# Attention over memory slots, then a three-way maxout layer: both softmaxes subtract their maximum

## The chip, the cores and the metric

The kernel runs on one core of a Trainium2 chip. The metric is the device time of one execution in microseconds (us); the time before is the median of three runs. One further execution was profiled, and all durations below come from that one. Engines have short names: PE is TensorE (matmuls), PEld its weight loads, DVE is VectorE, ACT is ScalarE, POOL is GpSimd, SP is SyncE, which here only issues DMAs. L499 is line 499 of the kernel's source.

## The reference, cut to what matters

```python
# q, k, v: (8, 8, 576, 64)   phi: (8, 8, 576, 32)   all float32
a = np.exp(phi - np.max(phi, axis=2, keepdims=True))   # axis 2: the tokens
a = a / (np.sum(a, axis=2, keepdims=True) + 1e-09)
k_m = np.einsum('bhsm,bhsd->bhmd', a, k)
v_m = np.einsum('bhsm,bhsd->bhmd', a, v)
scores = 1.0 / np.sqrt(64) * np.matmul(q, k_m.transpose(0, 1, 3, 2))
scores = scores - np.max(scores, axis=-1, keepdims=True)   # over the 32 slots
attn = np.exp(scores)
attn = attn / (np.sum(attn, axis=-1, keepdims=True) + 1e-09)
y = np.matmul(attn, v_m)                     # (8, 8, 576, 64)
x = y.transpose(0, 2, 1, 3).reshape(4608, 512)
h = np.maximum(np.maximum(x @ w1, x @ w2), x @ w3)     # w1, w2, w3: (512, 768)
out = h @ w_out                                        # w_out: (768, 512)
```

The first softmax runs over the 576 tokens of a head, the second over its 32 memory slots. Neither maximum changes the value of its softmax in exact arithmetic.

## The kernel before, in words

A batch (one of 8) holds 8 heads as 4 pairs and 576 tokens. The instructions of all engines are issued in an order written out by hand: a list of short words such as `F4@1!`, a letter for a step, a number for its part, the batch behind the `@`, and `!` or `*` to move an evacuation of PSUM to the other engine or to both. Each engine takes its share of the list strictly in that order. PSUM is eight banks of 512 fp32 columns; which banks a step takes is written out too, as a string of digits.

The steps of a batch:

- `L0`, `L1`, `L2`, `L3` (in halves `H`, `J`) load phi, k, v and q (L108, L111, L125). They are issued from POOL and cast to bf16 on the way, except phi, which stays fp32; the first phi comes from SP (L106). Each of k, v and q of a batch is 1.18 MB in HBM, phi is 0.59 MB.
- `E` (L262) is exp of phi on ACT, `B` (L282) sums phi's exponentials with k, v and a column of ones on PE, `N` (L300 to L314) normalizes on DVE, `K` (L329) transposes the result on PE. `r` (L117) repacks k and v on POOL for batches 2 to 7.
- `Q` (L344) transposes q in 32 x 32 blocks on DVE. `S` (L364) makes the scores of the batch on PE, two groups of 128 rows (slots of four heads) by 576 tokens, and exponentiates them on ACT (L373) straight from PSUM into a bf16 tile e2.
- For each group: `a` (L418) transposes e2 in 32 x 32 blocks, pairs of bf16 moved as one 4-byte element (288 columns); `s` (L426) sums over slots; `c` (L435) takes the reciprocal; `m` (L440) multiplies on POOL; `X` (L448) transposes back into attn. Batch 0 does it otherwise: `M` (L385) multiplies e2 with a block matrix of ones on PE, `R` takes exp(-ln) of the sums on ACT (L397, L403), and `X` multiplies on DVE (L408).
- The values are folded into the weights. `W` and `O` (with `o` for a half) form w3 times w_out, `V` (L246) turns w1 and w2 into w1 - w3 and w2 - w3, and `D0` to `D4` (L471) multiply the batch's values v_m with columns of these, to wp, and with w3 w_out, to wp3 (`D3`). So x @ w1 - x @ w3 is attn @ wp. For batch 0 `D1` to `D4` take other column ranges and subtract w3 within the product.
- `F0` to `F11` (L499) are the first layer, 6 tiles of 128 columns for w1 (even) and w2 (odd); `f` issues the first half ahead. The w1 half is evacuated with a ReLU on ACT or DVE (L195, L199), the w2 half with a maximum on DVE (L523) into hT. Each takes two banks.
- `T0` to `T4` (L542 to L571) are the output tiles of 128 tokens: six products of hT with w_out and two of attn with wp3; `p` issues two of the six ahead. The tile is copied from PSUM by ACT or DVE and written by one DMA from SP of 128 rows (L583). T4 belongs to two batches. The very last tile (L594 to L615) is in two column parts, 384 by SP and 128 by ACT.

The weights come once: w3 (`Y2`, 1.57 MB), w_out (`y4`, `y5`, 0.79 MB each), w1 in two parts (`y0` with 512 columns, 1.05 MB, and `y1`, 0.52) and w2 (`y2` with 256 columns, 0.52, and `y3`, 1.05). `Z` issues warm-up products on PE.

Of the kernel before, what the change touches and what calls it, by code (L numbers as in the profile page):

```python
# [8 lines left out]
FP32 = mybir.dt.float32  # L9
BF16 = mybir.dt.bfloat16  # L10
AF = mybir.ActivationFunctionType
ALU = mybir.AluOpType
# [3 lines left out]
def kernel(  # L16
# [139 lines left out]
    blkones = const.tile([P, P], BF16, name="blkones")  # L156
    nc.vector.memset(blkones, 0.0)
    for i in range(P // M):
        nc.vector.memset(blkones[M * i : M * (i + 1), M * i : M * (i + 1)], 1.0)
# [6 lines left out]
            02010240624567675420624062402640240264526720426206260402602460264301466410462046  # L166
            20462402472640320642026502642064026401460246046024604264026401462040640264026402
            64206420560272046042704624602642604264024062602032323232
# [85 lines left out]
    ln = const.tile([P, S], FP32, name="ln")  # L254
    ONES = {(0, 0), (0, 1)}
    st = {}

# [93 lines left out]
    def att_score(b):  # L351
# [3 lines left out]
        e2 = s["e2"] = work.tile([P, NG, S], BF16, name="e2")  # L355
# [16 lines left out]
        for a in range(NG):  # L372
            nc.scalar.activation(  # L373
                out=e2[:, a].rearrange("p (t r c) -> p t r c", t=2, c=NC),
                in_=sc[a][:, :, 0:SH].rearrange("p t (c r) -> p t r c", c=NC),
                func=AF.Exp,
                scale=0.125,
            )

    def ones_sum(b, g):  # L380
        s = st[b]
        e2 = s["e2"]
        sm = two_banks()
        for h in range(2):
            nc.tensor.matmul(  # L385
                sm[:, h, 0:SH],
                lhsT=blkones,
                rhs=e2[:, g, h * SH : (h + 1) * SH],
                start=True,
                stop=True,  # L390
            )
        s["sm", g] = sm

    def ones_rec(b, g):
        s = st[b]
        sm = s["sm", g]
        nc.scalar.activation(  # L397
            out=ln.rearrange("p (h n) -> p h n", h=2),
            in_=sm[:, :, 0:SH],
            func=AF.Ln,  # L400
        )
        r = work.tile([P, S], FP32, name="r")
        nc.scalar.activation(out=r, in_=ln, func=AF.Exp, scale=-1.0)  # L403
        s["r", g] = r

    def ones_mul(b, g):
        s = st[b]
        nc.vector.tensor_tensor(  # L408
            out=attns[b // 2][:, g, (b % 2) * S : (b % 2 + 1) * S],
            in0=s["e2"][:, g, 0:S],  # L410
            in1=s["r", g],
            op=ALU.mult,
        )

    def att_t(b, g):
        s = st[b]
        t = s["t", g] = work.tile([P, S // HP, R, 2], BF16, name="t", tag=f"t{g}")
        nc.vector.transpose(  # L418
            out=t.rearrange("p n r e -> p (n r e)").bitcast(FP32),
            in_=s["e2"][:, g].bitcast(FP32),  # L420
        )
# [109 lines left out]

    def ffn2_part(b, t, count):
# [19 lines left out]
    def ffn2(b, t, swap):  # L552
# [27 lines left out]
        r0 = (b // 2) * 2 * S + c0  # L580
        rows = out[r0 : r0 + P, :]
        evacuate("T", t, swap, ot, po)
        nc.sync.dma_start(out=rows, in_=ot)  # L583

    def ffn2_last(b, c0):
# [3 lines left out]
        r0 = (b // 2) * 2 * S + c0  # L589
        for i in range(2):  # L590
# [18 lines left out]
            rows = out[r0 : r0 + P, c]  # L609
            if i == 0:  # L610
                nc.vector.tensor_copy(out=ot[:, c], in_=po)
                nc.sync.dma_start(out=rows, in_=ot[:, c])
            else:
                nc.scalar.copy(out=ot[:, c], in_=po)  # L614
                nc.scalar.dma_start(out=rows, in_=ot[:, c])  # L615

    def issue(b, n, swap):
# [21 lines left out]
            "X": lambda: (ones_mul if (b, i) in ONES else att_back)(b, i),  # L639
            "M": lambda: ones_sum(b, i),  # L640
# [73 lines left out]
```

## Time and profile before

| what | value |
|---|---|
| median of 3 runs | 163.42 us (163.24 to 164.35) |
| profiled execution, device time | 163.54 us |
| its span in the profile | 161.8 us |
| idle before the first engine work, POOL | 0.24 us |
| 9.70 to 27.25 us: busy PE, DVE, ACT, POOL | 15.22, 8.32, 6.75, 5.89 us |
| 135.00 to 158.30 us: busy PE, DVE, ACT, POOL | 23.20, 10.86, 5.42, 0.00 us |
| issues of output DMAs | 36 from SP, 1 from ACT |

The span runs from the first to the last event that the profiler holds; the device time has 1.74 us more. A line of a group is the engine, operation and tile with its shape, how often it ran, the total busy time and the mean length of one in ns, then the idle time of the engine just ahead of it with what ended it. Busy times of one engine can overlap by some tens of ns from one instruction to the next, so that means times counts come to a little more than the busy total. In a timeline a bracket gives the idle time ahead of an instruction and what it waited for.

### The profile page before, as it was taken

How to read it: one execution, taken by the hardware profiler on the slowest of the kernel's cores; microseconds unless marked ns; L12 is line 12 of the kernel's file. 1: busy time of each engine (PE TensorE's matmuls, PEld its weight loads, DVE VectorE, ACT ScalarE, POOL GpSimd, SP SyncE). 2: the span in 40 equal slices, each digit the busy share in tenths (PEclk: the TensorE clock that was granted, in tenths of full speed). 3: DMA queues.
4: the chain of work that ended last, by engine and by line, in shares of the span. 5: the costliest groups of instructions: out<-in, count | busy, mean ns of one | idle time of the engine just before them, and what ended most of it. 6: DMA issues, size and time to landing. Idle time of an engine off the chain costs nothing.

```text
span 161.8 us, 4852 instructions
## 1 busy us (share of the span) xinstructions
PE 152.4 (94%) x2056; PEld 85.6 (53%) x2080; DVE 108.2 (67%) x208; ACT 87.8 (54%) x137; POOL 73.0 (45%) x76
## 2 busy tenths in 40 slices
PE   7978988999999999999999999999999999999991
PEld 2433643664476437645674567468533476754441
DVE  2013627797978687778899488988975978853111
ACT  0604408753685595667875787476397962501210
POOL 7931533430499259957959807946200820000000
PEclk9999999999999999999999999999999999999999
DMA  5999999999999999999999999999331311012333
GB/s 154 162 197 208 206 204 202 281 206 211 225 312 263 210 282 266 259 275 263 256 271 279 265 282 245 277 242 246 68 131 73 129 67 65 0 65 112 151 130 132
DMA packets 24086, 31.83 MB, mean 197 GB/s; under 512 B 2304, under 2 KB 18688, under 8 KB 24064
## 3 DMA queue, kind: packets, MB, share of 16 engines
q0 software_dynamic: 17184, 21.43, 69.9%
q1 hardware_dynamic: 5728, 9.96, 17.5%
q10 hardware_dynamic: 1152, 0.12, 0.8%
q8 instruction: 16, 0.26, 0.6%
q14 instruction: 6, 0.05, 0.1%
HBM read 39.38 MB, written 9.44 MB: 302 GB/s over the span
## 4 chain that ended last, share of the span: by engine, by line
PE 80%; DMA 15%; issue 2%; POOL 1%; ACT 0%; ACTq 0%; POOLq 0%
PE psum L499 30%; PE psum L542 28%; DMA w_sb<-in_moe_w_dram 11%; PE psum L562 9%; PE psum L471 5%; DMA kvo<-in_k_dram 5%; PE psum L282 3%; PE psum L364 2%; PE psum L571 1%; PE psum L329 1%; PE psum L594 1%; POOL kvo L111 1%; PE psum L602 0%; ACT wp L481 0%; ACT ot L614 0%
## 5 line engine op out<-in xcount | busy, mean ns | idle before, releaser
L499 PE MATMUL psum<-attn,wp 128*128 128x288 bf16 x384 | 50.8, 286 | 0.2
L542 PE MATMUL psum<-wo_sb,hT 128*128 128x512 bf16 x190 | 49.4, 379 | 1.4 <-issue 0.8
L499 PEld LDWEIGHTS <-wp 128*128 128x128 bf16 x384 | 36.7, 98 | 13.6 <-issue 1.1
L523 DVE TENSOR_TENSOR hT<-psum,h 128x576 bf16<-128x576 f32 x48 | 34.3, 748 | 5.6 <-PE psum L499 3.1
L117 POOL COPY kvr<-kvo 128x2304 bf16<-128x2304 bf16 x12 | 25.4, 2116 | 13.5 <-DMA kvo<-in_k_dram 9.2
L542 PEld LDWEIGHTS <-hT 128*128 128x128 bf16 x210 | 19.2, 98 | 22.5 <-issue 3.9
L195 ACT ACTIVATE h<-psum 128x576 bf16<-128x576 f32 x38 | 23.4, 651 | 11.9 <-PE psum L499 11.8
L197 ACT COPY ot<-psum 128x512 f32<-128x512 f32 x27 | 15.6, 591 | 24.4 <-PE psum L562 18.3
L440 POOL TENSOR_TENSOR t<-t,sm 128x576 bf16<-128x576 bf16 x14 | 16.1, 1158 | 25.9 <-DVE sm L435 25.9
L197 ACT CAST wp<-psum 128x1024 bf16<-128x1024 f32 (+1 forms) x18 | 17.3, 1003 | 2.4 <-PE psum L471 2.3
L562 PE MATMUL psum<-wp,attn 128*128 128x512 bf16 x61 | 17.9, 379 | 0.2
L184 PE MATMUL psum<-warm 128*128 128x512 bf16 x42 | 12.0, 440 | 1.4 <-DVE warm L153 1.2
L344 DVE STREAM_TRANSPOSE qT<-qq 128x576 f32<-128x576 f32 x16 | 11.9, 760 | 1.2 <-DMA qq<-in_q_dram 1.1
L201 DVE COPY ot<-psum 128x512 f32<-128x512 f32 x8 | 5.5, 682 | 9.4 <-PE psum L562 6.6
L373 ACT ACTIVATE e<-psum 128x576 bf16<-128x576 f32 x16 | 9.5, 649 | 3.9 <-PE psum L364 3.9
L262 ACT ACTIVATE e<-ph 128x1152 bf16<-128x1152 f32 (+1 forms) x9 | 9.4, 1055 | 3.0 <-DMA ph<-in_phi_dram 3.0
L482 DVE CAST wp<-psum 128x512 bf16<-128x512 f32 (+1 forms) x13 | 8.0, 644 | 3.9 <-PE psum L471 3.9
L426 DVE TENSOR_REDUCE sm<-t 128x18 f32<-128x576 bf16 x14 | 10.3, 738 | 0.3
L562 PEld LDWEIGHTS <-attn 128*128 128x128 bf16 x62 | 5.9, 98 | 7.0 <-issue 0.4
L125 POOL DMA_DIRECT2D qq<-in_q_dram x10 | 7.5, 747 | 4.4 <-DMA kvo<-in_k_dram 1.9
L282 PEld LDWEIGHTS <-e 64*32 64x32 bf16 x720 | 7.2, 90 | 3.5 <-issue 2.6
L199 DVE TENSOR_SCALAR h<-psum 128x576 bf16<-128x576 f32 x10 | 7.3, 740 | 2.1 <-PE psum L499 2.1
(61 smaller groups left out, 138.0 us busy)
## 6 DMA issues: line engine op xcount, KB each, us to landing
out_dram<-ot SPq DMA_DIRECT2D x35, 256.0 KB, 5.6
ph<-in_phi_dram POOLq DMA_DIRECT2D x7, 576.0 KB, 13.8
kvo<-in_k_dram POOLq DMA_DIRECT2D x7, 576.0 KB, 16.5
kvo<-in_v_dram POOLq DMA_DIRECT2D x7, 576.0 KB, 15.9
qq<-in_q_dram POOLq DMA_DIRECT2D x6, 576.0 KB, 12.8
qq<-in_q_dram POOLq DMA_DIRECT2D x4, 288.0 KB, 17.1
w_sb<-in_moe_w_dram POOLq DMA_DIRECT2D x2, 512.0 KB, 15.7
w_sb<-in_moe_w_dram POOLq DMA_DIRECT2D x1, 768.0 KB, 11.8
```

The source lines that it names most:

```text
L117: nc.gpsimd.tensor_copy(out=kvrs[b % 2][:, :, :, D * i : D * (i + 1)], in_=kv_of(b, i))
L184: nc.tensor.matmul(po[:, 0:BANK], lhsT=warm[:, 0:P], rhs=warm, start=True, stop=True)
L195: nc.scalar.activation(out=out_, in_=in_, func=AF.Relu)
L197: nc.scalar.copy(out=out_, in_=in_)
L282: nc.tensor.matmul(kvp[M * j : M * (j + 1), a, 0:nd], lhsT=s["e"][r, j, c, :], rhs=plain(r, j, c) if b < FULL else kvr[r, j, c, 0:nd], sta ...
L344: nc.vector.transpose(out=s["qT"][:, j].rearrange("p j c r e -> p (j c r e)").bitcast(FP32), in_=loaded[b]["q"][:, j].rearrange("p j c d - ...
L426: nc.vector.tensor_reduce(out=sm, in_=s["t", g].rearrange("p n r e -> p n e r"), op=ALU.add, axis=mybir.AxisListType.X,)
L440: (nc.vector if swap else nc.gpsimd).tensor_tensor(out=t, in0=t, in1=s["sm", g].unsqueeze(2).to_broadcast([P, S // HP, R, 2]), op=ALU.mult,)
L499: nc.tensor.matmul(acc[:, h, 0:SH], lhsT=wps[b][:, g, w * DF + ft * P : w * DF + (ft + 1) * P], rhs=attn[:, g, c0 : c0 + SH], start=(g == ...
L523: nc.vector.tensor_tensor(out=hT[:, ft, (b % 2) * S : (b % 2 + 1) * S].rearrange("p (h n) -> p h n", h=2), in0=a, in1=s["h1", ft], op=ALU.max,
L542: nc.tensor.matmul(po, lhsT=hT[:, fc, c0 : c0 + P], rhs=wo_sb[:, fc, :], start=(n == 0), stop=False,)
L562: nc.tensor.matmul(po, lhsT=attn[:, g, c0 : c0 + P], rhs=wp3s[b][:, g, :], start=False, stop=(g == NG - 1),)
```

## The change

Both softmaxes subtract their maximum.

- phi: `g` (phi_max) reduces phi over the 9 tokens that a partition holds, transposes in 32 x 32 blocks, reduces again, swaps neighbouring blocks of 32 partitions (two belong to a head), takes the larger and transposes it back. `h` (phi_sub) subtracts it in fp32, on POOL or, with `!`, on DVE.
- Scores: `S` leaves them in PSUM. For each group `a` transposes 576 fp32 columns from PSUM, `x` takes the maximum over the slots, `u` subtracts it on DVE or, with `!`, on POOL, and `e` exponentiates on ACT into the bf16 tile. `s`, `c`, `m`, `X` follow as before, now for batch 0 too; `M`, `R` and the ones matrix are gone.
- The tokens lie in another order in attn, so an output tile's rows are 64 and 64 rows of `out` at a stride of 9, and each tile is written by two DMAs.
- The order list and the banks are new.

```diff
-    blkones = const.tile([P, P], BF16, name="blkones")
...
+    def phi_max(b):
+        s = st.setdefault(b, {})
+        ph = loaded[b]["ph"]
+        top = work.tile([P, NP, M], FP32, name="top")
+        nc.vector.tensor_reduce(
+            out=top, in_=ph.rearrange("p j c m -> p j m c"), op=ALU.max, axis=mybir.AxisListType.X
+        )
+        turned = work.tile([P, NP, R], FP32, name="turned")
+        nc.vector.transpose(
+            out=turned.rearrange("p j r -> p (j r)"), in_=top.rearrange("p j m -> p (j m)")
+        )
+        mine = work.tile([P, NP], FP32, name="mine")
+        nc.vector.tensor_reduce(out=mine, in_=turned, op=ALU.max, axis=mybir.AxisListType.X)
+        other = work.tile([P, NP], FP32, name="other")
+        for i in range(P // R):
+            o = i ^ 1
+            nc.vector.tensor_copy(
+                out=other[R * i : R * (i + 1)], in_=mine[R * o : R * (o + 1)]
+            )
+        both = work.tile([P, NP, R], FP32, name="both")
+        nc.vector.tensor_tensor(
+            out=both,
+            in0=mine.unsqueeze(2).to_broadcast([P, NP, R]),
+            in1=other.unsqueeze(2).to_broadcast([P, NP, R]),
+            op=ALU.max,
+        )
+        s["top"] = work.tile([P, NP, M], FP32, name="tops")
+        nc.vector.transpose(
+            out=s["top"].rearrange("p j m -> p (j m)"), in_=both.rearrange("p j r -> p (j r)")
+        )
+
+    def phi_sub(b, swap):
+        ph = loaded[b]["ph"]
+        (nc.vector if swap else nc.gpsimd).tensor_tensor(
+            out=ph, in0=ph,
+            in1=st[b]["top"].unsqueeze(2).to_broadcast([P, NP, NC, M]),
+            op=ALU.subtract,
+        )
...
-        for a in range(NG):
-            nc.scalar.activation(
-                out=e2[:, a].rearrange("p (t r c) -> p t r c", t=2, c=NC),
-                in_=sc[a][:, :, 0:SH].rearrange("p t (c r) -> p t r c", c=NC),
-                func=AF.Exp,
-                scale=0.125,
-            )
-
-    def ones_sum(b, g):
...
-    def att_t(b, g):
-        s = st[b]
-        t = s["t", g] = work.tile([P, S // HP, R, 2], BF16, name="t", tag=f"t{g}")
-        nc.vector.transpose(
-            out=t.rearrange("p n r e -> p (n r e)").bitcast(FP32),
-            in_=s["e2"][:, g].bitcast(FP32),
-        )
+        s["sc"] = sc
+
+    def att_t(b, g):
+        s = st[b]
+        t = s["st", g] = work.tile([P, S // R, R], FP32, name="st", tag=f"st{g}")
+        nc.vector.transpose(
+            out=t.rearrange("p (t c) m -> p t (c m)", t=2), in_=s["sc"][g][:, :, 0:SH]
+        )
+
+    def att_max(b, g):
+        s = st[b]
+        mx = s["mx", g] = work.tile([P, S // R], FP32, name="mx", tag=f"mx{g}")
+        nc.vector.tensor_reduce(
+            out=mx, in_=s["st", g], op=ALU.max, axis=mybir.AxisListType.X
+        )
+
+    def att_sub(b, g, swap):
+        s = st[b]
+        t = s["st", g]
+        (nc.gpsimd if swap else nc.vector).tensor_tensor(
+            out=t, in0=t,
+            in1=s["mx", g].unsqueeze(2).to_broadcast([P, S // R, R]),
+            op=ALU.subtract,
+        )
+
+    def att_e(b, g):
+        s = st[b]
+        t = s["t", g] = work.tile([P, NC, R, 2], BF16, name="t", tag=f"t{g}")
         nc.scalar.activation(
+            out=t,
+            in_=s["st", g].rearrange("p (t c) m -> p c m t", t=2),
+            func=AF.Exp,
+            scale=0.125,
         )
...
+    def rows_at(b, c, d=slice(0, DM)):
+        return out[b * S : (b + 1) * S, d].rearrange("(t r c) d -> c r t d", t=2, c=NC)[c]
...
-        nc.sync.dma_start(out=rows, in_=ot)
+        if t < 4:
+            i = c0 // HP - (b % 2) * NC
+            for u in range(2):
+                nc.sync.dma_start(out=rows_at(b, i + u), in_=ot[HP * u : HP * (u + 1)])
...
-                nc.scalar.dma_start(out=rows, in_=ot[:, c])
+                for u in range(2):
+                    (nc.scalar, nc.sync)[u].dma_start(
+                        out=rows_at(b, at + u, c), in_=ot[HP * u : HP * (u + 1), c]
+                    )
...
-        E@0 H2@0 H0@0 L3@0 Z25@0 B0@0 I@0 N0@0 Z2@0 K0@0! Q0@0 Q1@0 Z9@0 S@0 Z2@0 M0@0 M1@0 R0@0
-        Y2@0 R1@0 W0@0 y4@0 W1@0 W2@0 Z6@0 o3@0 o0@0 H3@0 H1@0 o1@0 X0@0 y5@0 y0@0 o2@0 y2@0
-        B1@0 N1@0 y1@0 K1@0 O0@0! O3@0 O2@0! y3@0 O1@0 X1@0 D0@0* D3@0 D2@0 L0@1 F2@0 V0@0 F4@0!
...
+        L0@1 g@0 Z6@0 h@0! J0@1 Z25@0 H2@0 g@1 E@0 L3@0 J1@1 Q1@1 Q0@1 L1@1 H0@0 Q0@0 I@0 h@1
+        Q1@0 H3@0 H1@0 Y2@0 E@1 y4@0 y5@0 B0@1 N0@1 B0@0 Z9@0 N0@0 K0@0 S@0 y0@0 B1@0 a1@0 a0@0
+        K0@1! S@1 W1@0! y1@0 x0@0 x1@0 a0@1 u1@0 N1@0 W0@0 y3@0 e1@0 W2@0! u0@0! a1@1 x0@1 x1@1
+        s1@0 L0@2 o1@0 c1@0 y2@0 L2@1 Z2@0 e0@0 u0@1! u1@1! o3@0 e0@1 s0@0 e1@1 s0@1 c0@0 m0@0!
+        L1@2 c0@1 s1@1 c1@1 O3@0 m1@0! o2@0 m0@1 O2@0 O1@0! o0@0 X0@0 K1@0! X1@0 O0@0 D1@0 D0@0
+        D4@0 V2@0 m1@1 F6@0 F4@0 g@2 F10@0 F7@0 F5@0 F8@0! F0@0 F2@0 F9@0 D2@0 D3@0 B1@1 N1@1
...
```

## The prediction

> **What bounds the kernel now.** I read the page first, then the chain of waits in order of time, the timeline of the start, the busy time by stretch, and the groups by shape, which give the prices. The busy line:
>
> ```profile
> PE 152.4 (94%) x2056; PEld 85.6 (53%) x2080; DVE 108.2 (67%) x208; ACT 87.8 (54%) x137; POOL 73.0 (45%) x76
> ```
>
> A mean says little here; the chain says that there are two stages (start, length, what ran):
>
> ```profile
> 9.71 17.50 DMA w_sb<-in_moe_w_dram
> 27.25 0.41 PE psum L471 x16
> 27.66 3.05 PE psum L499 x24
> ...
> 157.86 0.34 PE psum L594 x6
> 158.38 0.27 ACT ot L614
> ```
>
> Until 27.25 us PE waits for loads, the last of them part y2 of w2; from there to the last matmul's end (158.30) PE is on the chain without a break. The stretches (length, then busy PE, PEld, DVE, ACT, POOL, clock, DMA):
>
> ```profile
> 27.25:158.30 131.05, 129.31 (x1760) 75.11 (x1780) 98.81 (x185) 78.29 (x122) 59.51 (x51) 1.00 0.85 200
> 45.00:135.00 90.00, 88.72 (x1293) 52.15 (x1307) 72.51 (x143) 62.15 (x96) 53.43 (x44) 1.00 0.94 221
> ```
>
> PE is 98.7% busy after 27.25; DVE, second, is busy for 72.5 of the 90 us in the middle, so it has 19% to spare there. These margins are what the change can use up. Two landings give the speed of the loads:
>
> ```profile
> 12.31 1.44 DVE L344 STREAM_TRANSPOSE qT<-qq 128x576 f32<-128x576 f32 x2 [1.08 <-DMA qq<-in_q_dram]
> ...
> 27.25 0.30 PE L471 MATMUL psum<-w_sb,kvt 64*32 64x256 bf16 x8 [0.66 <-DMA w_sb<-in_moe_w_dram]
> ```
>
> Both waits end with the landing. In issue order, counted as fp32 read from HBM, ph, k and q of batch 0 (2.95 MB) were in at 12.31 us; w3, w_out, v, y0 and y2 (another 5.90 MB) by 27.2 us. That is 5.90 MB in 14.9 us, 396 GB/s, with the DMA row of the page full throughout.
>
> The prices (busy, mean ns of one):
>
> ```profile
> L523 DVE TENSOR_TENSOR hT<-psum,h 128x576 bf16<-128x576 f32 x48 | 34.3, 748 | 5.6 <-PE psum L499 3.1 <-ACT h L195 2.1
> L117 POOL COPY kvr<-kvo 128x2304 bf16<-128x2304 bf16 x12 | 25.4, 2116 | 13.5 <-DMA kvo<-in_k_dram 9.2 <-DMA kvo<-in_v_dram 4.4
> L440 POOL TENSOR_TENSOR t<-t,sm 128x576 bf16<-128x576 bf16 x14 | 16.1, 1158 | 25.9 <-DVE sm L435 25.9
> L344 DVE STREAM_TRANSPOSE qT<-qq 128x576 f32<-128x576 f32 x16 | 11.9, 760 | 1.2 <-DMA qq<-in_q_dram 1.1
> L426 DVE TENSOR_REDUCE sm<-t 128x18 f32<-128x576 bf16 x14 | 10.3, 738 | 0.3
> L418 DVE STREAM_TRANSPOSE t<-e 128x288 f32<-128x288 f32 x14 | 6.3, 463 | 3.4 <-ACT e L373 3.4
> L304 DVE TENSOR_TENSOR kvn<-psum,rden 128x128 bf16<-128x128 f32 x8 | 2.3, 283 | 3.2 <-PE psum L282 3.0
> ```
>
> **The start: 10 us later.** In the changed order POOL issues ph, q and k of batch 1 (0.59 + 1.18 + 1.18 = 2.95 MB) ahead of v, w3, w_out and the parts of w1 and w2. The third fold of batch 0, D4@0, heads nearly all ffn1 work on PE and waits for y3 (1.05 MB), with y1 (0.52) before it; before, D2@0 waited for y2 (0.52), and y1 and y3 came while PE worked. So 2.95 + 0.52 + 1.05 - 0.52 = 4.00 MB more stand before PE's dense stage: 4.00 / 396 GB/s = 10.1 us, and D4@0 starts at 27.2 + 10.1 = 37.3 us. The bounds: 417 GB/s, as w3's 1.57 MB took from 12.31 to 16.08, gives 36.8; 353, all 8.85 MB from the chain's first load (2.13) to 27.2, gives 38.5.
>
> All other new work of the start fits below that. DVE: phi_max twice, phi_sub, four q transposes, and the score steps of two batches come to 27 us by the prices below, against 33 us between ph's landing (4 us) and 37.3. POOL waits once, for h@1, behind g@0, h@0 and g@1 on DVE (about 11 us); behind it stand the issues of v and of all weights, but seven earlier loads keep the DMA engines busy until 27.2 - (8.85 - 5.90)/0.396 = 19.8 us. Cost nothing; were h@1 done only at 20, each us beyond would be a us. The ones product, its Ln, Exp and multiply are dropped: 0.8 us of PE, 2.7 of ACT, 1.5 of DVE, all ahead of the landing, worth nothing.
>
> PE's dense work shrinks a little. Before, 131.05 us lay behind 27.25. Batch 1's B0 (0.80), K0 (0.28) and S (0.49) now run ahead of it, and D3 against D1 is left over, 0.1 less: 129.4 us. Alone, that ends PE at 37.3 + 129.4 = 166.7.
>
> **The middle: DVE passes PE.** Per batch DVE gains: phi_max, one reduce of 1152 (L344 less L418 is 1.03 ns per column; 738 ns for L426's 576 and as much for 576 more makes 1.33; bounds 1.18, the pace of w_sb's 2048-wide subtraction, and 1.48, twice L426), two 128-wide transposes (by the same 1.03 ns, 0.30 each), a reduce and a max of 128 (0.28 each by L304) and four small copies (0.1 each): 2.9 us. The scores' transposes are twice as wide: 2 x (0.76 - 0.46) = 0.6 (a PSUM source cannot make that free: L523 reads PSUM at the same pace). Two maxima at 0.74; subtraction on DVE for 5 of 16 groups, 0.75 each. Sum, reciprocal and back transpose are as before. Less: 2 ReLUs, 4 output copies and some wp halves that went to ACT, which at 54% has room.
>
> Counted from the instruction order, between D4@0 and the last score maximum of batch 5 (x1@5) DVE has: 26 evacuations of hT and h at 0.715 (18.6), 5 phi_max (14.5), 8 score transposes (6.1), 8 q transposes (5.9), 8 maxima (5.8), kvn five times (4.2), w_sb's subtractions (3.7), 5 sums and 4 reciprocals (4.7), 6 back transposes (2.6), 3 subtractions (2.2), folds and kvt (2.2): 70.5 us. The same count of the whole kernel before gives 113.6 against 108.2 busy, because neighbours overlap; with that factor, 67.2. PE has 58.6 in the same stretch, 56.9 from rows and 3% for its pauses. DVE is 8.6 us too long. PE can run ahead only as far as PSUM lets it: a half of ffn1 takes two of eight banks, and only DVE frees every second one; four halves of 0.5 us and a few output products, 2.5 us. So about 6.1 us of PE idle, and the rest of PE's work (70.8 us, with 51 us of DVE) follows dense: 166.7 + 6.1 = 172.8.
>
> ACT's exponentials now wait for a subtraction, and the ReLUs and copies that free PSUM stand behind them; ACT is 60% busy there, so this costs only where DVE is late, and that is counted.
>
> POOL gains six phi_sub in the dense stage (twice L440: 2.3; bound below 1.06, L117's pace) and eight score subtractions (1.16; below 0.53). It reaches 55 us in that 67 us stretch; the loads of later batches queue behind its waits for DVE. They used to land 12 to 16 us after issue with waits of at most 4.7 us, which the later pace covers: nothing, or up to 4.7.
>
> Here a rule speaks against the change. In the trace before, no DVE operation with two SBUF inputs ran beside POOL compute, so it is silent on this. The Trainium skill, "SBUF — State Buffer", section "SBUF: two separate sides", says that a DVE operation with two SBUF inputs and a GpSimd operation lock each other out for a whole instruction. What it would do here is the second rival.
>
> **The end: 0.5 us.** Output tiles leave as two DMAs of 64 rows: SP issues 71 at 0.33 us, 24 us in all, beside PE. The rows are 2 KB as before, scattered. The last 128 columns now leave partly as a third SP issue, 0.68 us after DVE's copy instead of 0.17 on ACT's queue. Each issue waits for the landing of the eighth before it, four tiles or 6.9 us in the tail, against 1.9 to 7.6 now: nothing, at most 0.7.
>
> **Sum.** Span 172.8 + 3.5 (as 158.3 to 161.8) + 0.5 = 176.8. The profiled execution took 163.54 for a span of 161.8, 1.74 around it, and is 0.12 over the median: 178.5, less 0.12, **178.4 us**, 9% slower.
>
> **Rivals.**
> - *DVE keeps up* (0.22). The reduces come out shorter, or PE finds enough queued output products. Only the late start stays: 166.7 + 4.0 + 1.6 = 172.3 us. For it: 10.3 us of output products begun early (p) are spread over this stretch. Against it: DVE's 8.6 us too many.
> - *DVE and POOL block each other* (0.17). In the dense stage POOL computes in 64 of 130 us (12 kvr copies 25.4, 13 products 15.1, six phi_sub 13.8, eight subtractions 9.3), in pieces of 1.2 to 2.3 us. If it holds up DVE's ten operations with two SBUF inputs (four subtractions, the maximum in six phi_max) and the copies of six phi_max, that is 16 places, each 1 us half of the time: 8 us on the engine that decides, 186.4 us. It decides once DVE's sm or st steps stand beside POOL's in the timeline with stretched times.
> - *The loads ride along* (0.04). If the DMA engines had room, the extra 4 MB would land with the others and the dense stage would start at 27.2 with 1.6 us less work; with DVE keeping up the time is 163.4 - 1.6 + 0.5 = 162.3, not slower. It needs 12.85 MB in 25.1 us, 512 GB/s, and decides from y3's landing before 28.2. Against it, 396 to 417 seen.
>
> **Numbers.** My forecast has 0.52, its own range 175 to 182 (no running ahead and a late landing, 182; twice the running ahead and an early one, 175); 0.05 is left for what I did not think of. The range goes from the first rival with the landing at 36.8, no cost at the end and half of PE's 1.74 us of pauses (172.3 - 0.5 - 0.5 - 0.9 = 170.4) to the second with the late landing (186.4 + 1.2 = 187.6). A measurement of this kernel tells about 1%, 1.6 us. Slower by more: 0.94; within: 0.04; faster: 0.02.
>
> **What would show it.** D4@0's first matmul should wait for a w_sb load until 37 us (36.8 to 38.5); DVE should be over 95% busy from 40 to 105 us with PE losing some 6 us there, behind hT and kvn; DVE's total near 144 us; phi_max's wide reduce 1.2 to 1.5 us; PE dense again after 110; last matmul to span end 4 us. Wrong would be a dense stage that starts before 34, PE idle of under 3 us in the middle, or POOL as releaser of most waits.

## The result and the profile after

The changed kernel takes 203.5 us (median of 4 runs, 203.29 to 205.81) against 163.5 us (163.24 to 164.35) for the kernel before on the same chip: 1.247 times as long, interval 1.237 to 1.257. The forecast was 178.4 us with a range up to 187.6. The direction was right; the size was short by 25.1 us. The profiled execution took 203.29 us for a span of 201.5. Times below are medians of all of a kernel's runs; the ratios (with their 95% intervals) leave out single runs that took over 1.5% longer than the fastest of the same kernel.

The busy line of the page after (engine, busy us, share of the span, instructions):

```profile
PE 162.3 (81%) x2076; PEld 88.0 (44%) x2076; DVE 159.2 (79%) x289; ACT 96.5 (48%) x142; POOL 105.0 (52%) x94
```

DVE has gained 51 us and POOL 32. PE, which has 0.8 us of products less to do, is busy for 10 us more: TensorE's granted clock was not full all the time. The busy time by stretch, from the landing that D4@0 waits for (39.41 us) to the end of the last score maximum of batch 5, x1@5 (122.82), and from there to the last matmul's end (length, then busy PE, PEld, DVE, ACT, POOL, clock, DMA share, GB/s):

```profile
39.41:122.82 83.41, 68.60 (x998) 37.32 (x999) 76.35 (x141) 47.73 (x70) 57.63 (x45) 0.94 0.99 198
122.82:197.40 74.58, 69.11 (x673) 38.62 (x671) 55.14 (x94) 36.68 (x56) 23.04 (x17) 0.98 0.41 94
```

These are the terms of the prediction's sum. It had the landing at 37.3 and x1@5 done on DVE 67.2 us later, with PE 2.5 us of work ahead by then (so 61.1 us of PE's work and 6.1 of idle), and 70.8 - 2.5 = 68.3 us of PE's work behind that, which ends PE at 172.8. Measured: 39.41, 83.41, 74.58, which ends it at 197.40. So 2.1 us of the excess came before D4@0, 16.2 in the middle and 6.3 behind x1@5, 24.6 together; the stretch from the last matmul to the end of the span is 4.1 us, where 4.0 was expected.

Where PE stops, in its timeline (start, length, what resumed; in the bracket the idle time ahead of it and what ended it):

```profile
39.41 0.41 PE L496 MATMUL psum<-w_sb,kvt 64*32 64x512 bf16 x8 [1.45 <-DMA w_sb<-in_moe_w_dram]
...
62.06 0.66 PE L524 MATMUL psum<-attn,wp 128*128 128x288 bf16 x2 [2.14 <-DVE kvn L354]
...
82.36 0.71 PE L403 MATMUL psum<-qT,kvt 32*32 32x288 bf16 x32 [2.38 <-DVE qT L384]
...
133.82 0.29 PE L369 MATMUL psum<-ident,kvn 128*128 128x128 bf16 x1 [5.24 <-DVE kvn L344]
```

Seven stops of over 1 us lie between 45 and 134 us, 18.4 us in all, and DVE ends every one of them. The six over 2 us stand behind a phi_max that DVE works off in one piece of 4.2 us or more.

The prices after, against those the prediction used (groups by shape, mean ns of one after the busy time):

```profile
L291 POOL TENSOR_TENSOR ph<-ph,tops 128x1152 f32<-128x1152 f32 x7 | 18.4, 2627 | 20.8 <-DVE tops L285 20.8
L257 DVE TENSOR_REDUCE top<-ph 128x128 f32<-128x1152 f32 x8 | 17.2, 2147 | 3.5 <-DMA ph<-in_phi_dram 3.5
...
L274 DVE COPY other<-mine 32x4 f32<-32x4 f32 x32 | 9.4, 294 | 0.6
L431 DVE TENSOR_TENSOR st<-st,mx 128x576 f32<-128x576 f32 x5 | 6.0, 1209 | 0.1
L242 DVE TENSOR_TENSOR w_sb<-w_sb 128x1024 bf16<-128x1024 bf16 x2 | 2.8, 1424 | 0.0
```

The wide reduce is 2.15 us and not 1.33. The other three DVE rows are means over very unlike times: most of the small copies take 0.16 us and one took 3.93; the score subtractions run from 0.72 to 2.66; the 1024-wide weight subtraction, 0.68 before, took up to 2.17. What the long ones have in common is seen by laying two timelines side by side. DVE:

```profile
127.86 0.28 DVE L268 TENSOR_REDUCE mine<-turned 128x4 f32<-128x128 f32 x1
128.18 4.46 DVE L274 COPY other<-mine 32x4 f32<-32x4 f32 x4
132.68 0.29 DVE L278 TENSOR_TENSOR both<-mine,other 128x128 f32<-128x128 f32 x1
```

and POOL in the same microseconds:

```profile
126.67 2.26 POOL L465 TENSOR_TENSOR t<-t,sm 128x576 bf16<-128x576 bf16 x2
128.88 2.10 POOL L117 COPY kvr<-kvo 128x2304 bf16<-128x2304 bf16 x1
130.94 1.15 POOL L465 TENSOR_TENSOR t<-t,sm 128x576 bf16<-128x576 bf16 x1
```

The first of four copies, which need 0.6 us together, ends only when POOL's unbroken run ends, at 132.1: it took 3.93 us. This is the place of PE's longest stop, 5.24 us up to 133.82.

The clock has a pattern of its own. In stretches of 3.41 us laid on one grid (length, busy PE, granted clock, DMA share, GB/s):

```profile
58.47:61.88 3.41, 1.46 (x16) 1.00 1.14 281
61.88:65.29 3.41, 3.23 (x42) 0.51 1.19 224
78.95:82.36 3.41, 1.04 (x13) 1.00 1.02 158
82.36:85.77 3.41, 3.41 (x39) 0.51 0.77 173
92.60:96.01 3.41, 1.56 (x20) 1.00 1.13 214
96.01:99.42 3.41, 2.61 (x20) 1.00 0.89 245
```

In this execution a stretch in which PE was busy for 1.46 us or less is followed by one at half clock; 1.56 us was enough to keep the clock full. Four such spells lie behind 40 us (61.9, 82.4, 113.1 and 133.6), each 3.4 us long; at half clock that is up to 1.7 us of PE's work lost each, 6.8 us in all. The kernel before has none.

### The profile page after: what moved, and what is told of

Same layout as the page of the kernel before. It is cut to its first block, busy times and chain, and to the rows that moved or that the text cites. A ratio compares the mean times of both kernels' runs of the same rounds, so it can differ in the third digit from the quotient of the medians.

```text
span 201.5 us, 5013 instructions
## 1 busy us (share of the span) xinstructions
PE 162.3 (81%) x2076; PEld 88.0 (44%) x2076; DVE 159.2 (79%) x289; ACT 96.5 (48%) x142; POOL 105.0 (52%) x94
## 4 chain that ended last, share of the span: by engine, by line
PE 45%; DVE 34%; DMA 10%; POOL 4%; issue 3%; ACT 2%; SPq 0%; DVEq 0%; ACTq 0%
PE psum L571 17%; PE psum L524 17%; DMA w_sb<-in_moe_w_dram 8%; DVE top L257 8%; PE psum L591 5%; DVE other L274 5%; DVE hT L548 5%; DVE w_sb L242 2%; DVE sm L451 2%; PE psum L496 2%; DMA ph<-in_phi_dram 2%; DVE st L417 1%; DVE qT L384 1%; PE psum L403 1%; POOL ph L291 1%
## 5 line engine op out<-in xcount | busy, mean ns | idle before, releaser
L524 PE MATMUL psum<-attn,wp 128*128 128x288 bf16 x384 | 52.6, 288 | 7.3 <-DVE kvn L354 4.8
L571 PE MATMUL psum<-wo_sb,hT 128*128 128x512 bf16 x210 | 56.7, 402 | 1.7 <-DVE hT L548 1.7
L524 PEld LDWEIGHTS <-wp 128*128 128x128 bf16 x384 | 37.3, 98 | 22.4 <-issue 10.3
L193 ACT COPY ot<-psum 128x512 f32<-128x512 f32 x31 | 18.2, 591 | 34.7 <-PE psum L591 25.3
L291 POOL TENSOR_TENSOR ph<-ph,tops 128x1152 f32<-128x1152 f32 x7 | 18.4, 2627 | 20.8 <-DVE tops L285 20.8
L193 ACT CAST wp<-psum 128x1024 bf16<-128x1024 f32 (+1 forms) x25 | 24.1, 1008 | 4.3 <-PE psum L496 4.3
L431 POOL TENSOR_TENSOR st<-st,mx 128x576 f32<-128x576 f32 x11 | 12.6, 1155 | 18.3 <-DVE mx L424 18.3
L257 DVE TENSOR_REDUCE top<-ph 128x128 f32<-128x1152 f32 x8 | 17.2, 2147 | 3.5 <-DMA ph<-in_phi_dram 3.5
L591 PE MATMUL psum<-wp,attn 128*128 128x512 bf16 x62 | 19.1, 391 | 0.0
L417 DVE STREAM_TRANSPOSE st<-psum 128x576 f32<-128x576 f32 x16 | 11.7, 762 | 6.7 <-PE psum L403 6.7
L441 ACT ACTIVATE t<-st 128x576 bf16<-128x576 f32 x16 | 12.8, 812 | 2.5 <-POOL st L431 2.2
L496 PE MATMUL psum<-w_sb,kvt 64*32 64x512 bf16 (+1 forms) x200 | 9.4, 374 | 4.9 <-DVE st L417 2.3
```

What stands on the lines that cost most here:

```text
L193: nc.scalar.copy(out=out_, in_=in_)
L257: nc.vector.tensor_reduce(out=top, in_=ph.rearrange("p j c m -> p j m c"), op=ALU.max, axis=mybir.AxisListType.X,)
L291: (nc.vector if swap else nc.gpsimd).tensor_tensor(out=ph, in0=ph, in1=st[b]["top"].unsqueeze(2).to_broadcast([P, NP, NC, M]), op=ALU.subt ...
L417: nc.vector.transpose(out=t.rearrange("p (t c) m -> p t (c m)", t=2), in_=s["sc"][g][:, :, 0:SH])
L524: nc.tensor.matmul(acc[:, h, 0:SH], lhsT=wps[b][:, g, w * DF + ft * P : w * DF + (ft + 1) * P], rhs=attn[:, g, c0 : c0 + SH], start=(g == ...
L571: nc.tensor.matmul(po, lhsT=hT[:, fc, c0 : c0 + P], rhs=wo_sb[:, fc, :], start=(n == 0), stop=False,)
```

## The experiments

Theory after the first look: DVE cannot keep up, because phi_max costs more than I had put (the wide reduce, and standing still beside POOL), and its unbroken stretch stops PE, which then also loses its clock. Rivals: the score maxima are the cost; the order and the late start are; the chain through phi_sub on POOL is; it is the sum of DVE's work and not the unbroken stretch.

**One part of the change alone.** Three kernels leave out `g` and `h`, or `x` and `u`, or all four (the maxima are then not subtracted).

```diff
-            "g": lambda: phi_max(b),
-            "h": lambda: phi_sub(b, swap == "!"),
+            "g": lambda: None,
+            "h": lambda: None,
```

> Leaves out the maximum of phi and its subtraction (steps g and h); the order of all else is kept. Theory A: what costs is phi_max as one unbroken piece of 4.2 us on DVE, which stands in front of hT, kvn and qT and which PE cannot bridge. Then PE's pauses between the first D4 and 138 us (20.3 us in the changed kernel) shrink to under 8 us, the half-clock time (about 14 us at 0.5 from 39 to 138) nearly goes, D4@0 starts near 37.3 instead of 39.4: 176 to 181 us. Theory B: only the sum of DVE's work counts (159.2 us busy); 34 us less of it is about two thirds of what was added: 185 to 190 us.

> Leaves out the maximum of the scores and its subtraction (steps x and u); the transposes of the scores in fp32 stay. DVE has 17 us less, POOL 12.6 us less. Theory A (phi_max's unbroken pieces): little changes, 196 to 201 us. Theory B (the sum of DVE's work): a third of what was added goes, 190 to 193 us. A third theory, that DVE and POOL hold each other up: less POOL work beside DVE, the 3.9 us stop of the small copies at 128 us goes, 190 to 196 us.

> Leaves out both maxima and both subtractions; the new order, the early loads of batch 1, the wide transposes and the two output DMAs stay. If the start costs what the loads ahead of y3 cost (4.00 MB at 396 GB/s, D4@0 at 37.3) and PE's dense work follows with its old pauses: 172 to 174 us, which was the first rival's time. If the new order itself is poor (banks, waits on PE without DVE being late): 176 or more. If the late start is due to phi_max holding up POOL's issues: D4@0 before 35, under 171.

Without phi's maximum 178.6 us (1.093 times before, 1.089 to 1.097), without the scores' 196.0 (1.201, 1.197 to 1.204), with neither 175.3 (1.074, 1.071 to 1.078), 3 us above the 172.3 of the prediction's first rival. So the new order with its early loads costs about 12 us, the scores' maxima 3.3 on top of that, and phi's maximum 20.6 on top of the order and 24.9 on top of the rest. The stretches of the kernel without phi's maximum, cut at the same two places:

```profile
37.12:105.30 68.18, 62.30 (x995) 36.44 (x998) 58.76 (x99) 48.57 (x71) 46.78 (x42) 1.00 1.13 237
105.30:172.80 67.50, 66.94 (x665) 38.31 (x671) 47.64 (x85) 36.61 (x56) 20.51 (x16) 1.00 0.49 110
```

Full clock throughout, no stop above 1.43 us in the middle, and D4@0 at 37.12. This is nearly the kernel that the prediction described.

**The stopped copies.** The four copies became reduces over one element, which move the same values.

```diff
-            nc.vector.tensor_copy(
-                out=other[R * i : R * (i + 1)], in_=mine[R * o : R * (o + 1)]
-            )
+            nc.vector.tensor_reduce(
+                out=other[R * i : R * (i + 1)],
+                in_=mine[R * o : R * (o + 1)].unsqueeze(2), op=ALU.max, axis=mybir.AxisListType.X,
+            )
```

> The four small copies of phi_max (L274) become four reduces over one element, the same values. Theory C: the copies stopped for 3.9 us at 128 us, and 0.5 us at 94, because a POOL instruction was running and this kind of copy cannot run beside it; a reduce can. Then no L274 instruction is over 0.4 us, PE's pause of 5.2 us at 134 falls to about 2, and the time falls by 3 to 6 us: 197 to 200. If the stop has another cause (its input, DVE's queue): the same 3.9 us stop, 203 to 204.

202.1 us (1.237, 1.233 to 1.241). The reduces take 0.145 to 0.151 us and none is stretched, but the next operation, the maximum of two SBUF tiles, stood still in their place (DVE's timeline):

```profile
129.44 3.41 DVE L281 TENSOR_TENSOR both<-mine,other 128x128 f32<-128x128 f32 x1
```

So a copy and an operation with two inputs from SBUF are held up, a reduce is not, and taking one of two out gained 1.4 us at most, where the theory had 3 to 6.

**The stride.** The wide reduce reads the 1152 values as they lie. It then takes maxima over nine neighbours and not over the nine tokens of a slot. What is subtracted is still the same number for all tokens of a slot, so the softmax keeps its value, but it is not the maximum that the change asks for: the run prices the stride and is no repair that could stay.

```diff
-            in_=ph.rearrange("p j c m -> p j m c"),
+            in_=ph.rearrange("p j c m -> p (j c m)").rearrange("p (j m c) -> p j m c", j=NP, m=M),
```

> The wide reduce of phi_max reads the same 1152 values of each partition in the order in which they lie (so it takes the maximum over nine neighbours instead of over the nine tokens of a memory slot; the subtracted values differ, nothing else does). Theory: the stride of 128 bytes between the values of one maximum makes it 2.15 us instead of the 1.33 that I had put; then each of the eight takes 1.2 to 1.4 us, the unbroken stretch of phi_max falls from 4.2 to 3.4 us, and the kernel to about 195 to 200 us (8 times 0.8 us of VectorE, most of it in front of a waiting TensorE, and perhaps a spell of half clock less). Rival: the reduce is that slow whatever the order (its 1152 fp32 inputs, or the 128 outputs, cost 2.1 us): then the row stays at 2.1 and the time within 0.5% of 203.5.

196.9 us (1.207, 1.204 to 1.211), 6.6 us less. The row:

```profile
L257 DVE TENSOR_REDUCE top<-ph 128x128 f32<-128x1152 f32 x8 | 10.6, 1328 | 3.6 <-DMA ph<-in_phi_dram 3.6
```

1.33 us is what I had put for the strided one. Eight times 0.82 is 6.6 us of DVE's time, and the kernel got shorter by as much. Half clock behind 40 us fell from 13.7 to 6.8 us as well, up to 3.4 us of PE's work, so not all of the gain need be the reduce's own time; some of that was outside the stretch where DVE decides.

**The early loads alone**, in the kernel before:

```diff
-        Y2@0 R1@0 W0@0 ...
+        L0@1 J0@1 J1@1 L1@1 Y2@0 R1@0 W0@0 ...
```

> The kernel before with the four loads of batch 1 (scores of the memory slots, both halves of q, and k; 2.95 MB) moved ahead of the load of the first weight, and nothing else. Theory of my first step: the weights come later by these bytes at 396 GB/s, 7.4 us, TensorE has nothing else to do there, so 163.3 becomes 169 to 171. Rival (the loads ride along in gaps of the DMA engines, or TensorE's later work makes up for it): 163 to 165.

172.05 us (1.055, 1.050 to 1.060): 8.7 us, 1 more than the theory's upper end. In PE's timeline the first transposes of w3, which began at 16.08 before, now wait for their load:

```profile
23.91 2.74 PE L209 MATMUL psum<-ident,w_sb 128*128 128x128 bf16 x24 [8.28 <-DMA w_sb<-in_moe_w_dram]
```

That is 7.8 us later (7.4 expected). PE was at half clock from 18.9 to 29.1 us here, which it was not before; that would account for the other 0.9, but was not tried apart. The later loads are not hidden and PE does not make up for them.

**Idle products in two stops.** `fill` writes products of the zero tile into the bank that the next step takes.

```diff
-  ... Q0@3 D0@3 S@3 ...      N@6 m0@4 m1@4 K@6! ...
+  ... Q0@3 D0@3 z10@3 S@3 ...   N@6 m0@4 m1@4 z20@6 K@6! ...
```

> The kernel after with idle products on the zero tile put in front of the two places where TensorE stopped and then ran at half clock: ten ahead of the scores of batch 3 (the stop of 2.4 us at 82), twenty ahead of the transposes of batch 6 (the stop of 5.2 us at 134). They write into the bank that the next operation takes. Theory: the stops stay, since they are VectorE's, but the two spells of half clock behind them vanish, each worth 1.7 us: 199.5 to 201. Rival: the half clock does not come from the stops (it falls anyway at other times), or costs nothing because VectorE is the later of the two after it: 203 to 205.

201.5 us (1.235, 1.229 to 1.240), 0.5 above the theory's range. No spell of half clock follows the two filled stops, but the grid lay elsewhere in this execution (its spells begin at 28.2, 45.3, 96.5 and 113.6, all on one grid of 3.41 us), and the stops at 46.0 and 95.8, which had kept their clock in the kernel after, lost it now. By these two executions a stop costs its clock by where it falls in the grid, so filling two of seven does not save two spells.

**phi_max in pieces.** Its twelve operations (the wide reduce by pair of heads) are issued one by one behind other steps, for batches 2 to 7.

```diff
+        steps[b] = ([lambda j=j: wide(j) for j in range(NP)] + [turn, narrow]
+            + [lambda i=i: copy(i) for i in range(P // R)] + [join, back])
...
+        if n[0] in "FDTXaxK" and steps:
+            at = min(steps)
+            steps[at].pop(0)()
```

> The kernel after with phi_max of batches 2 to 7 cut into twelve pieces (the wide reduce by pair of heads, then each further operation) that are issued one by one behind other operations of the list, with the rest ahead of phi_sub; the same work, plus three more instructions for each batch. Theory (the unbroken stretch is what stops TensorE, and the stop is what drops the clock): the stops of over 2 us ahead of 138 us become smaller than 1.5, the spells of half clock go, and the time is 190 to 197. Rival (VectorE's sum alone sets the time of the middle: 90 us busy of 98.6): the stops are spread out instead, 200 to 204.

205.0 us (1.253, 1.246 to 1.260), above the times of both theories. The stops at the old places went, ten of 0.8 to 3.3 us came at others, and there are five spells of half clock. But four of the new stops are behind ACT or POOL, the longest too: with the last piece, phi_sub, exp and B came later. So the test was not clean, and the next two repeat it with nobody waiting for phi_max.

**phi_max with its result unused**, in one piece and in pieces (phi_sub left out):

```diff
-            "h": lambda: phi_sub(b, swap == "!"),
+            "h": lambda: None,
```

> The kernel after without phi_sub: phi_max runs where it did, in one piece, but nothing uses its result (phi is exponentiated as it comes). So VectorE has the whole of phi_max's work, and no chain phi_max, phi_sub, exp, B hangs on it. Without both it was 178.6, with both 203.5. Theory (VectorE's time for phi_max is what costs): 196 to 203. Rival (the chain through GpSimd's subtraction is what costs, VectorE has room): 179 to 186.

> As e10_max_unused, with phi_max of batches 2 to 7 cut into twelve pieces that stand behind twelve other operations, and nobody waiting for the last piece. Same work of VectorE. If the unbroken stretch of 4.2 us is what stops TensorE, this is 8 us or more below e10_max_unused, since the stops of over 2 us go and with them the spells of half clock. If it is the sum of VectorE's work, it is within 3 us of e10_max_unused. The first spread version did not get shorter (205.0), but there phi_sub, exp and B came later with the last piece, which this one leaves out.

213.4 us (1.304, 1.299 to 1.310) and 204.9 (1.252, 1.245 to 1.258). The second is 8.5 us below the first, as the theory of the unbroken stretch had it, but the first is no fair measure. Neither of its theories had expected it: it leaves out 18 us of POOL's work and is 10 us slower than the kernel after. Its DVE (the profiled execution took 216.9 us):

```profile
99.07 0.28 DVE L268 TENSOR_REDUCE mine<-turned 128x4 f32<-128x128 f32 x1
99.39 7.02 DVE L274 COPY other<-mine 32x4 f32<-32x4 f32 x4
```

and POOL there:

```profile
99.01 0.81 POOL L108 DMA_DIRECT2D ph<-in_phi_dram  x1
...
101.29 0.76 POOL L111 DMA_DIRECT2D kvo<-in_k_dram  x1
102.02 4.18 POOL L117 COPY kvr<-kvo 128x2304 bf16<-128x2304 bf16 x2
```

In the kernel after, POOL's subtraction, which waits for phi_max, stands here between POOL's loads and its copies, so that the copies run when DVE's small ones are done. Now four load issues and two copies run back to back beside them, and three of DVE's four small copies stand still in turn, for 2.2, 2.6 and 2.0 us. DVE is busy for 169.6 us in place of 159.2, and for 163.6 in the version in pieces, so most of the 8.5 us between the two can be DVE standing still and need not be the unbroken stretch.

**Half of the packs.** The copies of k and v on POOL are left out for batches 4 to 7 (their B reads what batches 2 and 3 left).

```diff
-            "r": lambda: pack(b, i),
+            "r": lambda: pack(b, i) if b < 4 else None,
```

> The kernel after without the repacking of k and v on GpSimd for batches 4 to 7 (their B reads what batches 2 and 3 left in the tile): 8 copies of 2.18 us, 17.4 us of GpSimd, are left out. Theory of the lock (a copy or a subtraction on VectorE stands still while GpSimd computes): the copy of 3.9 us at 128 falls to 0.2, the stop of TensorE behind it from 5.2 to about 2 us, with the spell of half clock behind it gone: 197 to 200. Rival (the stretched copy is an accident of the order and GpSimd's work has no share in VectorE's): the copy stays long, 202 to 204.

198.3 us (1.215, 1.210 to 1.220), as the theory had it. In the same place of DVE's timeline:

```profile
128.19 0.69 DVE L274 COPY other<-mine 32x4 f32<-32x4 f32 x4
```

The stop of PE behind it fell from 5.24 to 1.46 us, the spell of half clock there is gone.

**phi_sub later in POOL's queue**, behind the issues of v, w3 and w_out:

```diff
-        ... H0@0 Q0@0 I@0 h@1 Q1@0 H3@0 H1@0 Y2@0 E@1 y4@0 y5@0 B0@1 ...
+        ... H0@0 Q0@0 I@0 Q1@0 H3@0 H1@0 Y2@0 y4@0 y5@0 h@1 E@1 B0@1 ...
```

> The kernel after with batch 1's phi_sub (and the exp that needs it) moved behind the issue of v, w3 and the output weights in GpSimd's queue. Theory (the wait of phi_sub for VectorE's phi_max, 7.0 us of idle time on GpSimd up to 14.5 us, held back the loads behind it, and put the start of the dense stage at 39.4 instead of 37.3): the wait of D4@0 for its weights ends at 37.0 to 37.6 and the time is 201 to 202. Rival (batch 1 becomes late by it, and the stage is held by VectorE anyway): D4@0 at 37.5, but 203 to 205.

D4@0 starts at 37.26 without a wait, so the cause of the late start is found. The time does not tell the two theories apart: 203.3 us over all four runs is the rival's, 202.4 without the longest lies between them (1.241, 1.232 to 1.249). In the profiled execution five spells of half clock lie behind 40 us and not four, and the stop of 5.2 us is unchanged.

**No operation in phi_max that can stand still**: copies and maximum as reduces with one input, the two values side by side in one tile.

```diff
+        pair = work.tile([P, NP, 2], FP32, name="pair")
...
+                out=pair[R * i : R * (i + 1), :, 1], in_=pair[R * o : R * (o + 1), :, 0:1],
...
-        nc.vector.tensor_tensor(
-            out=both, in0=mine.unsqueeze(2).to_broadcast([P, NP, R]), ...
+        nc.vector.tensor_reduce(
+            out=both, in_=pair.unsqueeze(2).to_broadcast([P, NP, R, 2]), ...
```

> The kernel after with both kinds of operation of phi_max that stood still beside GpSimd replaced: the four copies and the maximum of two tiles become reduces with one input (the two values of a pair lie side by side in one tile). Same result, same count of operations. Theory (only copies and operations with two inputs from SBUF are held up, reduces and transposes are not): the copy row falls from 9.4 to 4.7 us, no operation of phi_max is stretched, the stop of TensorE at 134 us falls from 5.2 to under 2 us and the spell of half clock behind it goes: 197 to 200. Rival (whatever stands there next is held up instead, as in the run with the copies alone replaced): a transpose or reduce of 2 us or more beside GpSimd's copies, 201 to 204.

198.6 us (1.213, 1.206 to 1.221), the theory's. The rows (busy us, mean ns):

```profile
L273 DVE TENSOR_REDUCE pair<-pair 32x4 f32<-32x4 f32 x32 | 4.8, 149 | 0.6
L280 DVE TENSOR_REDUCE both<-pair 128x128 f32<-128x256 f32 x8 | 3.4, 420 | 0.3
```

Nothing in phi_max is stretched, and nothing else took the stop over. PE's stop at the end of the middle is 1.54 us.

**The same, unused, in one piece and in pieces.**

> As e10_max_unused (phi_max in one piece, its result unused, no phi_sub), with the reduces of e13_no_stop in it. Theory (the 213.4 of e10_max_unused came from VectorE standing still, since GpSimd's copies run back to back there): phi_max's rows have no stretched operation any more, and the time falls by 7 us or more, to 198 to 206; what stays is the stretched subtraction of the weights (6.4 us for two). Rival (phi_max without phi_sub is slow for another reason): 210 to 214.

> As e15_no_stop_unused, with phi_max of batches 2 to 7 in twelve pieces behind other operations. Both have the same work and nobody waits for it, so the difference is what the unbroken stretch costs by itself. Theory (stretch): 6 us or more below e15_no_stop_unused. Rival (sum): within 2 us of it.

198.0 us (1.207, 1.198 to 1.217) and 197.8 (1.210, 1.202 to 1.219). The first is 15.4 us under its twin with copies, so the excess of those 213.4 was DVE standing still. It is also within 0.6 us of the version that does use the result (198.6): the chain through phi_sub on POOL, the rival of the first run with the result unused, costs next to nothing. Between the two there is no difference, as the rival had it. But the version in pieces has 3.3 us more of DVE's work (reduces by pair of heads 19.1 us against 17.2, and the weight subtractions, which met POOL elsewhere, 7.9 against 5.2): one weight subtraction of 1.2 us took 5.25 beside POOL, and PE stopped for 5.49 us behind it. So this pair does not settle what an unbroken stretch costs by itself.

**The three changes together**: no stops, contiguous read, phi_sub later. It is called the repaired kernel below, though with the contiguous read it does not subtract the maximum that was asked for.

> The three repairs together: e13_no_stop, the contiguous read of e5_contig_reduce (with its maximum over neighbours) and the later phi_sub of e9_late_sub. VectorE's work is then what my sum had put for phi_max. If the three terms were all that I had sized wrongly, 203.5 - 6.6 - 5 - 1, 189 to 192, and what is left above 178.4 is the pauses that I had counted at 6 us and the half clock. If the pauses follow VectorE's work more than one for one, 180 to 188.

189.24 us (1.156, 1.150 to 1.163), within the range for terms that add up. Cut at the same two places:

```profile
37.35:114.59 77.24, 64.48 (x998) 36.54 (x999) 73.56 (x144) 48.84 (x71) 59.37 (x46) 1.00 1.03 209
114.59:183.30 68.71, 67.76 (x673) 38.22 (x671) 50.48 (x94) 36.69 (x56) 23.05 (x17) 1.00 0.47 108
```

D4@0 starts where the prediction had it, no stop is longer than 2.1 us, and the clock is full from 24 us on. Behind x1@5 it takes 68.7 us, where 68.3 were forecast. What is left above the forecast is the 10.0 us in the middle: DVE is busy for 73.56 us there and not 67.2, since the score and weight subtractions still stand still beside POOL (3.9 us more than their prices, by rows) and phi_max's rows are 1.7 above theirs, and it idles for 3.7. No version beats the kernel before: even the one without any maximum is 12 us slower.

## Why the prediction was wrong, step by step

**The start: the mechanism right, one term missing.** 37.3 was forecast; the order without phi's maximum gives 37.12, and with phi_sub moved 37.26. I costed h@1's wait on POOL at nothing, since seven earlier loads would keep the DMA engines busy until 19.8 us. The trace after has POOL idle for 7.04 us until phi_max of batch 1 is done, phi_sub from 14.50 for 2.62 us, and the loads behind it at 17 us and later: D4@0 2.1 us late. The earlier loads did not cover that: from 18 to 24 us the DMA engines moved 120, 175 and 138 GB/s in three stretches of 2 us, and with phi_sub moved 205, 209 and 214.

**The middle: the step that failed.** I had DVE as the bound of D4@0 to x1@5, which it is: it is busy for 76.35 of 83.41 us there. But the sum for it, 67.2 us of work and no pause, was 9.2 us short on the work. By rows of this stretch: five wide reduces 10.7 us against 6.7 (stride); the copies 3.7 against 2.0 (0.5 of that by two that stood still beside POOL's load issues, the rest because one takes 0.16 us and not 0.1); the score subtractions 4.6 against 2.2 and the weight subtractions 5.2 against 3.7 (both stand still beside POOL); 9.6 together; the rest of phi_max is as forecast within 0.3. The other rows are 2.5 above their prices, and neighbours overlap by 2.9 more than I had taken off, which nearly cancels. I had used for a strided reduce the pace of rows whose inputs lie together. The Trainium skill, "Advanced Engine Details and Errata", section "SBUF Cachelines", says that an access which takes another 16-byte line each time pays a penalty, without a figure; the runs agree and give it for this reduce, 2.15 against 1.33 us.

**The pauses of DVE were put at nothing.** I had DVE work off its 67.2 us without a break, with PE 2.5 us ahead of it at the end. The lead was there: without phi's maximum PE had 62.30 us of products done by x1@5 at full clock, where I had counted 58.6 before that place of the order. But DVE idles for 7.1 of the 83.41 us, 4.7 of them in waits for PE's products (3.4 for the scores that it transposes), and still for 3.7 in the repaired kernel (77.24 less 73.56). PE and DVE wait for each other in turn, and a stretch with DVE busy for 91.5% (after) to 95% (repaired) is as full as it got here. This is the other 7.1 of the middle's 16.2 us.

**Behind x1@5** PE was to be dense for 68.3 us. It took 74.58, with the 5.24 us stop and a spell of half clock of 1.7 in it; repaired 68.71. So PE's work was counted rightly there, and what was missing is mostly the stop behind the one copy that stood still, with the spell of half clock after it.

**The lock was made a rival, and it was a term.** Its mechanism is what happened: in place of 16 places of 1 us half of the time, three operations of 0.16 to 0.72 us took 2.2 to 3.9, and few others stood still for shorter. Its price in this kernel is about 5 us for phi_max (203.5 less 198.6), and it comes on top of the forecast, not in its stead. The range ended at 187.6 because it held the cases apart; they held together. The rule quoted in the prediction, the Trainium skill, "SBUF — State Buffer", section "SBUF: two separate sides", agrees in kind: a score subtraction of 0.72 us that met a POOL copy of 2.1 took 2.66. Its section "Who interferes with whom" adds what sorted the experiments, that a reduce never contends and a copy can.

**The clock was not in the sum at all**: up to 6.8 us of PE's work in the profiled execution. It is no term beside those above, since the spells lie within these stretches, three of them where DVE decides; how much of the time they cost was not taken apart.

**The rivals.** DVE keeps up fell: DVE fills 91.5% of the middle and PE loses 13.1 us there in six stops behind it; even repaired, with 6.4 us more work than forecast, DVE fills 95% and D4@0 to x1@5 takes 77.2 us. The loads riding along fell (8.7 us in the kernel before). **POOL** cost nothing as a chain, as forecast, but phi_sub at 2.63 us was above my 2.3. **The end** was right: 4.1 us against 4.0.

What stays open: without the scores' maxima DVE has 65.0 us of work in a stretch of 77.4 (to the last transposed scores of batch 5), so DVE's sum does not set every version's time by itself; two spells of half clock explain at most 3.4 us of that, the rest I have not taken apart.

## What to carry to other kernels

Count the second engine of a kernel that is full with the first one at its strided and contended prices: the stride of an operand was worth 0.82 us of 2.15 on one reduce, and eight reduces without it (though not of the same values) took 6.6 us off the time. Where GpSimd computes beside VectorE, look for the longest unbroken run of GpSimd and for copies or two-input operations on VectorE that can meet it, and write those as one-input reduces; taking work away from GpSimd can move what is left of it beside them and make it worse, as in the run of 213.4 us. Mechanisms that all have the profile on their side are terms of one sum, not alternatives.

## What the runs showed of the hardware that was not expected

- What a VectorE copy loses beside GpSimd can outlast one GpSimd instruction: one of 0.16 us ended after 3.93, with a run of three instructions. Elsewhere three copies in turn waited for 2.2, 2.6 and 2.0 us within one run, and a subtraction of two SBUF inputs (0.72 us alone) got in after the first of two back-to-back instructions, in 1.16 us. A reduce or a 32 x 32 transpose was never stretched in these runs, and the copies written as reduces took 0.15 us in the middle of such a run.
- The clock falls and rises on a grid of 3.41 us that lies differently in each execution and holds through it (in the kernel after all ten edges are within 0.13 us of one grid). The Trainium skill, "TensorE: Matmul & The Clock Gate", section "What's actually happening", has this window as free-running; its section "HAM oscillation — how this bites in real kernels" warns of idle gaps over some 3.4 us. Here stops of 2.1 to 2.4 us were enough, where they fell for the most part within one stretch of the grid: in the kernel after, busy for 1.04 to 1.46 us of 3.41 lost the clock, 1.56 kept it. On the same grid a run with the copies replaced shows the other side of it at 96 us:

```profile
92.60:96.01 3.41, 1.30 (x7) 1.00 1.04 216
96.01:99.42 3.41, 3.39 (x15) 0.51 0.94 254
```

where the kernel after, with 1.56 us in that stretch, stayed at full clock.

The busy time of one stretch does not give a bound that holds for all runs. With the later phi_sub a stretch with 1.34 us kept the clock:

```profile
79.60:83.01 3.41, 1.34 (x36) 1.00 1.12 196
83.01:86.42 3.41, 3.41 (x24) 1.00 0.39 111
```

and with phi_max in pieces one with 1.64 us lost it:

```profile
74.49:77.90 3.41, 1.64 (x19) 1.00 0.05 15
77.90:81.31 3.41, 1.66 (x74) 0.51 0.02 5
```

What decides between the two is not shown.
